# Two layers of attention and gated MLP on one core: shared score passes, zero-weight matmuls in idle TensorE slots, w_sp transposed once, and a spatial sum in four passes

## The chip, the cores and the metric

The kernel runs on one core of one Trainium2 chip. The metric is the device time of one launch in microseconds (us), as the median of several runs. The profile's span, from the first to the last instruction of the core, is about 2 us shorter (2191.0 us where the run took 2192.77). "Granted clock" is the share of TensorE's full clock that the chip allowed, averaged over a stretch; PE is TensorE, ACT is ScalarE, DVE is VectorE, SP is the engine that issues most DMAs (transfers between memories). PSUM is the memory that TensorE writes into, in banks. A "fill" is the group of score matmuls that fills PSUM for one exponential; a "value product" multiplies exponentials by V; "side work" is all else on TensorE: projections, the mixer, the spatial sum. "Warm" and "cold" stand for full and half clock. A "stretch" is a window of time, in us from the start of the span.

## The reference, cut to what matters

```python
# S = 2048 tokens, D = 512, 32 heads of 16, one key and value head shared by all; all bf16
def attention(x):                        # called on the layer-normed x, added to x
    q = (x @ wq).reshape(S, 32, 16)
    k = x @ wk;  v = x @ wv              # [2048, 16] each
    p = softmax(q . k * 16 ** -0.5)      # 32 x 2048 x 2048 scores
    return (p @ v).reshape(S, 512) @ wo
def mixer(x):                            # called on the layer-normed x, added to x
    z = gelu(x @ w_in)                   # [2048, 1792]
    z1, z2 = z[:, :896], layernorm(z[:, 896:])
    g = w_sp @ z2 + b_sp[:, None]        # w_sp is 2048 x 2048: the "spatial sum" over tokens
    return (z1 * g) @ w_out
x = x + attention(ln(x)); x = x + mixer(ln(x)); x = x + attention(ln(x)); x = x + mixer(ln(x))
```

Each layer has 134 million scores. The kernel treats them as 2048 blocks of 128 keys by 512 (query, head) columns; over two layers that is 4096 blocks, and every block needs an exponential.

## The kernel before

The program is generated in Python by a list scheduler. It knows a duration for every operation, simulates the five engines, and fixes the order of each engine's instructions. On the chip that order is static; semaphores only hold an instruction until its inputs are there.

Score blocks are filled by TensorE in PSUM and then take one of two ways. ScalarE takes groups of three or two blocks and applies its exponential; VectorE takes single blocks and builds an exponential from seven arithmetic operations on pairs of blocks.

```python
self.chunks = [512, 512, 512, 256, 128, 128]   # query tokens per chunk; the mixer of a chunk follows its attention
self.passes = [(0, 8, 1), (8, 12, 2)]          # spatial sum: token tiles 0-7 after chunk 1, 8-11 after chunk 2
self.s_fin = 12                                # the final pass sums tiles 12-15 and finishes the layer
self.ring = [(0, 3), (3, 2)]                   # PSUM banks of ScalarE's fills: 3 and 2, alternating
self.pvb = 6                                   # one bank for the value product
sc = self.sc = Sched([5, 7])                   # only two spare banks for all side work and VectorE's fills
sc.streams["pe"] = [self.fill_s, self.pv_s, self.dx_s]

def _qk(self, e, b, bank):                     # one score block: 32 rows of the array, row group j
    for s, kt in enumerate(b.unit.kts):
        ins = e.matmul(self.b32(bank)[:, s * n:(s + 1) * n], self.kT[32 * j:32 * j + 32, kt * 128:(kt + 1) * 128],
                       self.qs[32 * j:32 * j + 32, g.qslot, 0:n], tile_position=(32 * j, 0), start=True, stop=True)

# FillStream: ScalarE's 3 or 2 blocks (priority 0)      DexStream: VectorE's block by itself (priority 2.5)
o = sc.op("pe", lambda e: k.qk(e, b, j.bank.idx), 0.27, deps, 2.5, sem="dfill", job=j, first=True)

# ... spatial(): for every 256 tokens tc and every tile s of the pass, a transposing load of 64 KB
ld = self.dma(lambda e, sl=sl, s=s, tc=tc: e.dma_start_transpose(
    self.wsT[:, sl, :], self.w_sp_d[tc * 256:(tc + 1) * 256, s * 128:(s + 1) * 128]), self.last_ws[sl] or [], ...)
if final: todo.append(("b", None))             # the bias, as a matmul
if acc:   todo.append(("g", None))             # the earlier passes' sum gp, added with an identity matmul
todo += [("w", w) for w in ws]
# not final: DVE copies PSUM to gp.  final: DVE multiplies PSUM by z1, then the product with w_out
```

In the final pass of a layer one "group" is six 128x256 matmuls (bias, identity, four tiles); there are 56 per layer. A group of an earlier pass has no bias.

The softmax here doesn't subtract the row's maximum and nothing guards it: scores larger than these inputs give would overflow.

## Time and profile before

| before | |
|---|---|
| time | 2193.21 us median (2191.41 to 2195.01, 2 runs) |
| ScalarE busy, VectorE busy, TensorE busy | 80%, 82%, 87% |
| mean granted TensorE clock | 0.747 |
| blocks exponentiated by ScalarE, VectorE | 3570, 526 |
| TensorE's wait for w_sp loads | 43.1 us, 20.6 of it at the boundary and 22.5 at the end |

To find where the time goes I cut the span at four marks: the first exponential on ScalarE, the end of the first layer's last GELU, the last copy into V for the second layer (from then on the second attention runs freely), and the end of the second layer's last GELU.

| stage (us) | start | attention 1 | boundary | attention 2 | end | sum |
|---|---|---|---|---|---|---|
| before | 29.6 | 939.4 | 170.6 | 914.2 | 137.2 | 2191.0 |

The page of the kernel before: busy time of each engine with its share of the span, then lines of busy tenths in 40 equal slices of the span (PEclk: granted clock in tenths), then the chain of work that ended last.

```profile
PE 1910.1 (87%) x16492; PEld 722.1 (33%) x16580; DVE 1792.7 (82%) x3228; ACT 1759.3 (80%) x1544; POOL 58.9 (3%) x104
...
PE   7999897998799989987888888878897999899778
...
DVE  7988899988899998953359999989989998988423
ACT  7999899988999998942149999999989999978300
...
PEclk8555595556799997788885557866668998965879
...
PE 47%; ACT 30%; issue 11%; DVE 8%; SPq 2%; DMA 1%; POOL 1%; ACTq 0%; DVEq 0%
ACT Pa L1111 28%; PE ps_all L1321 16%; PE ps_all L1166 9%; PE ps_all L923 7%; PE ps_all L652 3%; PE ps_all L967 2%; PE ps_all L796 2%; PE ps_all L921 2%; PE ps_all L817 2%; DVE E L1272 2%; SPq L888 1%; PE ps_all L918 1%; ACT z2n L836 1%; DVE gp L936 1%; DMA wsT<-in_B_w_sp_dram 1%
```

ScalarE and VectorE show 9 for most of the two attentions, and fall to 1 to 4 in slices 22 to 24 and at the end: those are the boundaries. TensorE is 7 to 9 everywhere, but PEclk is 5 in the early part of both attentions, where attention runs without side work. A busy TensorE at half clock is not a fast one: 32x512 score matmuls last 0.605 us on average where the clock is 0.5, and 0.384 us where it is 1.0. The chain (shares of the span, by engine and then by line) is mostly TensorE and ScalarE handing over to each other.

Groups of instructions of the kernel before (busy us, mean ns | idle before, and who ended it). L1111 is ScalarE's exponential, L1321 the score matmul, L1272 the first of VectorE's seven operations:

```profile
L1111 ACT ACTIVATE Pa<-ps_all 128x1536 bf16<-128x1536 f32 (+2 forms) x1429 | 1646.1, 1265 | 132.8 <-PE ps_all L1321 116.4
L1321 PE MATMUL ps_all<-qs,kT 32*128 32x512 bf16 (+2 forms) x6148 | 835.5, 392 | 161.2 <-ACT Pa L1111 142.5
...
L1272 DVE TENSOR_SCALAR E<-ps_all 128x512 int32<-128x512 f32 x526 | 349.5, 684 | 44.3 <-PE ps_all L1321 42.6
```

ScalarE was held up 116.4 us by score matmuls, VectorE 42.6 us. From the view of waits, TensorE's matmuls and its loads of weights (PEld), each with total us, times and longest us:

```profile
PE ps_all L918 <- DMA wsT<-in_B_w_sp_dram: 43.1, 8, 8.9
PEld ps_all L918 <- DMA wsT<-in_B_w_sp_dram: 6.5, 1, 6.5
```

The timeline of TensorE near the end of the kernel (start, us, what; in brackets the idle time before it and its cause):

```profile
2064.64 0.60 PE L923 MATMUL ps_all<-wsT,z2n 128*128 128x256 bf16 x4
2065.08 0.27 PE L921 MATMUL ps_all<-gp,ident 128*128 128x256 bf16 x1
2065.19 0.60 PE L923 MATMUL ps_all<-wsT,z2n 128*128 128x256 bf16 x4
2074.71 0.37 PE L918 MATMUL ps_all<-b_11,ident 8*128 8x256 bf16 x1 [8.92 <-DMA wsT<-in_B_w_sp_dram]
2075.01 0.39 PE L921 MATMUL ps_all<-gp,ident 128*128 128x256 bf16 x1
2075.20 1.06 PE L923 MATMUL ps_all<-wsT,z2n 128*128 128x256 bf16 x4
2076.19 0.39 PE L918 MATMUL ps_all<-b_11,ident 8*128 8x256 bf16 x1
```

TensorE stands still 8.92 us for a transposing load, and the groups after the wait run at half clock: from one L918 to the next 1.48 us, where warm groups take 0.86 (41 of them in this trace).

### The profile page before, as it was taken

The numbers are of one execution on the slowest core, as the hardware profiler recorded it, in microseconds if no ns is written. First come the engines' busy times: TensorE is split into PE (matmuls) and PEld (weight loads), VectorE is DVE, ScalarE is ACT, GpSimd is POOL, SyncE is SP. The second block draws the span as 40 slices with busy tenths as digits, with TensorE's granted clock in tenths as the row PEclk, the third lists the DMA queues.
The fourth block names the chain that finished last, engine by engine and source line by source line (L and its number), as shares of the span: only waits on it lengthen the run. The fifth ranks groups of instructions, "written<-read, shape, count | busy, mean of one in ns | idle before, by whom it ended". The sixth has DMA issues, their size and how long they took to land.

```text
span 2191.0 us, 39478 instructions
## 1 busy us (share of the span) xinstructions
PE 1910.1 (87%) x16492; PEld 722.1 (33%) x16580; DVE 1792.7 (82%) x3228; ACT 1759.3 (80%) x1544; POOL 58.9 (3%) x104
## 2 busy tenths in 40 slices
PE   7999897998799989987888888878897999899778
PEld 3111221122244335554431112211222443465444
DVE  7988899988899998953359999989989998988423
ACT  7999899988999998942149999999989999978300
POOL 2000000000000000000000000000000000000000
PEclk8555595556799997788885557866668998965879
DMA  2000001000001010021100000010000110100312
GB/s 93 1 1 1 1 1 37 1 1 1 18 21 29 12 30 15 3 71 37 28 21 1 1 1 1 1 37 1 1 1 18 25 25 1 38 12 2 75 51 72
DMA packets 108402, 42.97 MB, mean 20 GB/s; under 512 B 79288, under 2 KB 107712, under 8 KB 108224
## 3 DMA queue, kind: packets, MB, share of 16 engines
q1 hardware_dynamic: 108224, 40.44, 7.2%
q8 instruction: 130, 2.13, 0.4%
q14 instruction: 48, 0.39, 0.1%
HBM read 14.19 MB, written 9.44 MB: 11 GB/s over the span
## 4 chain that ended last, share of the span: by engine, by line
PE 47%; ACT 30%; issue 11%; DVE 8%; SPq 2%; DMA 1%; POOL 1%; ACTq 0%; DVEq 0%
ACT Pa L1111 28%; PE ps_all L1321 16%; PE ps_all L1166 9%; PE ps_all L923 7%; PE ps_all L652 3%; PE ps_all L967 2%; PE ps_all L796 2%; PE ps_all L921 2%; PE ps_all L817 2%; DVE E L1272 2%; SPq L888 1%; PE ps_all L918 1%; ACT z2n L836 1%; DVE gp L936 1%; DMA wsT<-in_B_w_sp_dram 1%
## 5 line engine op out<-in xcount | busy, mean ns | idle before, releaser
L1111 ACT ACTIVATE Pa<-ps_all 128x1536 bf16<-128x1536 f32 (+2 forms) x1429 | 1646.1, 1265 | 132.8 <-PE ps_all L1321 116.4
L1321 PE MATMUL ps_all<-qs,kT 32*128 32x512 bf16 (+2 forms) x6148 | 835.5, 392 | 161.2 <-ACT Pa L1111 142.5
L1166 PE MATMUL ps_all<-Pa,V 128*32 128x512 bf16 (+2 forms) x5369 | 517.9, 396 | 7.5 <-DVE oT L675 4.6
L1321 PEld LDWEIGHTS ps_all<-qs,kT 32*128 32x128 bf16 x6148 | 224.0, 101 | 733.0 <-ACT Pa L1111 484.7
L1272 DVE TENSOR_SCALAR E<-ps_all 128x512 int32<-128x512 f32 x526 | 349.5, 684 | 44.3 <-PE ps_all L1321 42.6
L1306 DVE SCALAR_TENSOR_TENSOR Pd<-E 128x1024 uint16<-128x1024 int32 x263 | 319.6, 1215 | 0.6
L923 PE MATMUL ps_all<-wsT,z2n 128*128 128x256 bf16 x1792 | 281.2, 291 | 5.1 <-DVE E L1272 2.1
L1166 PE MATMUL ps_all<-Pd,V 128*32 128x512 bf16 (+2 forms) x775 | 263.1, 403 | 0.0
L1166 PEld LDWEIGHTS ps_all<-Pa,V 128*32 128x32 bf16 x5369 | 134.1, 103 | 339.2 <-issue 278.9
L923 PEld LDWEIGHTS ps_all<-wsT,z2n 128*128 128x128 bf16 x1792 | 173.9, 103 | 62.6 <-issue 22.2
L1301 DVE TENSOR_TENSOR E<-E 128x1024 f16<-128x1024 f16 x263 | 180.0, 684 | 2.5
L1304 DVE TENSOR_TENSOR E<-E 128x1024 f16<-128x1024 f16 x263 | 179.8, 684 | 2.4
L1295 DVE TENSOR_SCALAR E<-E 128x1024 f16<-128x1024 uint16 x263 | 179.7, 685 | 1.2
L945 DVE TENSOR_TENSOR E<-ps_all,z1s 128x512 bf16<-128x512 f32 (+1 forms) x64 | 39.9, 624 | 124.3 <-PE ps_all L923 115.1
L1298 DVE TENSOR_SCALAR E<-E 128x1024 f16<-128x1024 f16 x263 | 110.3, 420 | 2.4
L1297 DVE TENSOR_SCALAR E<-E 128x1024 f16<-128x1024 f16 x263 | 110.2, 419 | 1.3
L652 PE MATMUL ps_all<-xnTA,wq_pad 128*128 128x512 bf16 (+2 forms) x347 | 93.7, 383 | 11.7 <-issue 7.0
L542 ACT ACTIVATE xnTA<-ps_all 128x1024 bf16<-128x1024 bf16 x13 | 13.1, 1023 | 109.8 <-PE ps_all L533 109.8
L936 DVE CAST gp<-ps_all 128x512 bf16<-128x512 f32 (+1 forms) x128 | 78.4, 618 | 22.9 <-PE ps_all L923 22.3
L661 DVE CAST qs<-ps_all 128x512 bf16<-128x512 f32 (+2 forms) x94 | 47.6, 506 | 52.1 <-PE ps_all L652 51.7
L796 PE MATMUL ps_all<-w_in_r,xnTB 128*128 128x448 bf16 x256 | 77.5, 424 | 1.6 <-DVE E L1272 0.7
L918 PE MATMUL ps_all<-b_11,ident 8*128 8x256 bf16 x112 | 35.3, 315 | 48.9 <-DMA wsT<-in_B_w_sp_dram 43.1
(68 smaller groups left out, 1123.6 us busy)
## 6 DMA issues: line engine op xcount, KB each, us to landing
z1s<-z_scratch SPq DMA_DIRECT2D x16, 448.0 KB, 4.0
z_scratch<-z1s SPq DMA_DIRECT2D x6, 896.0 KB, 4.3
wsT<-in_B_w_sp_dram SPq DMA_TRANSPOSE x256, 2.4
X<-in_A_x_dram SPq DMA_DIRECT2D x8, 256.0 KB, 5.2
out_dram<-X SPq DMA_DIRECT2D x16, 128.0 KB, 1.9
w_in_r<-in_B_w_in_dram SPq DMA_DIRECT2D x1, 1792.0 KB, 9.9
E<-in_B_w_out_dram SPq DMA_DIRECT2D x2, 896.0 KB, 6.8
z_scratch<-z1s SPq DMA_DIRECT2D x2, 448.0 KB, 3.5
```

Source lines behind the costliest of these rows:

```text
L652: ins = e.matmul(self.b32(b)[:, 0:n], self.wq_pad[:, kd, g.hg, :], self.xnTA[:, kd, g.t0:g.t0 + n], start=(kd == 0), stop=(kd == KD - 1))
L796: ins = e.matmul(self.b32(b)[:, 0:448], self.xnTB[:, kd, i * 128:(i + 1) * 128], self.w_in_r[:, kd, FH + h * 448:FH + (h + 1) * 448], star ...
L923: ins = e.matmul(o_, self.z2n[:, w[0], f * 128:(f + 1) * 128], self.wsT[:, w[1], :], start=st, stop=sp_)
L1111: return e.activation(k.Pa[:, base:base + n, :], k.b32(b0, n).rearrange("p (k q) -> p k q", k=n), ACTF.Exp, scale=SCALE)
L1166: ins = e.matmul(k.b32(k.pvb)[32 * j:32 * j + 32, 0:n], k.V[:, kt, 32 * j:32 * j + 32], b.slot[:, s * n:(s + 1) * n], tile_position=(0, 32 ...
L1272: c = sc.op("dve", lambda e: e.tensor_scalar(k.eI[:, s, 512 * i:512 * (i + 1)], k.b32(j.bank.idx)[:, 0:512], C_LOG2, C_BIAS, op0=ALU.mult, ...
L1295: return lambda e: e.tensor_scalar(out, a, m, None, op0=ALU.mult)
L1298: return lambda e: e.tensor_scalar(out, a, m, b, op0=ALU.mult, op1=ALU.add)
L1301: o4 = sc.op("dve", lambda e: e.tensor_tensor(q, u, w, ALU.mult), d_sb(1024, 0.521e-3), [o3], pr)
L1304: o6 = sc.op("dve", lambda e: e.tensor_tensor(q, q, u, ALU.mult), d_sb(1024, 0.521e-3), [o5], pr)
L1306: o7 = sc.op("dve", lambda e: e.scalar_tensor_tensor(po.bitcast(U16), I, 2.0 ** -9, q, op0=ALU.mult, op1=ALU.add), d_sb(1024, 1.042e-3), [ ...
L1321: ins = e.matmul(self.b32(bank)[:, s * n:(s + 1) * n], self.kT[32 * j:32 * j + 32, kt * 128:(kt + 1) * 128], self.qs[32 * j:32 * j + 32, g ...
```

## The change

Its intent: keep TensorE's clock up through attention, take VectorE's separate score matmuls out of TensorE's time, and free the boundaries of transposing loads and left-over work. The core of the diff:

```diff
+TICK = 3.4133
+TICK_COLS = 3060.0
...   # the scheduler's model: below TICK_COLS array-weighted columns in a step, the next step is slow
+    def fast(self, t):
+        return self.tick.get(int(t / TICK) - 1, 0.0) >= TICK_COLS
...   # idle TensorE slots
+class WarmStream:
+        t = sc.below(f, TICK_COLS + WARM)        # WARM = 250
+        if not sc.fast(t):
+            return (t, -1.0)                      # cold: before everything else
+        return (t, 0.6)                           # warm: after fills and value products, before side work
+                ins = e.matmul(k.b32(k.pvb)[:, 0:n], k.zero[:], k.wo_r[:, 0, 0:n], start=False, stop=False)
...   # VectorE's block x joins ScalarE's fill, in a row group that the fill leaves free
+        x = k.dx_s.take(t, [b.j for b in blocks])
             for i, b in enumerate(blocks):
                 ins = k.qk(e, b, b0 + i)
+            if x is not None:
+                ins = k.qk(e, x, j.bank.idx)
-        o = sc.op("pe", lambda e: k.qk(e, b, j.bank.idx), 0.27, deps, 2.5, sem="dfill", job=j, first=True)
...   # w_sp: 16 transposes of 512 KB into the buffer gp, stored to DRAM, during chunk 0
+            tr = self.dma(lambda e, s=s: e.dma_start_transpose(stg[:, s % 7, :], self.w_sp_d[:, s * 128:(s + 1) * 128]), ...)
+            st = self.dma(lambda e, s=s: e.dma_start(self.ws_d.ap()[s], stg[:, s % 7, :]), [tr], ...)
...   # then plain loads of up to four tiles
-                ld = self.dma(lambda e, ...: e.dma_start_transpose(self.wsT[:, sl, :], ...))
+            ld = self.dma(lambda e, ...: e.dma_start(
+                self.wsT[:, 4 * sl:4 * sl + s1 - s0, :], self.ws_dv[:, s0:s1, tc * 256:(tc + 1) * 256]), ...)
...   # four passes; the middle ones add in SBUF with VectorE, no identity matmul
-        self.passes = [(0, 8, 1), (8, 12, 2)]
+        self.passes = [(0, 4, 0), (4, 8, 1), (8, 12, 2)]
-                    if acc:
+                    if final:
                         todo.append(("g", None))
+                        if acc:
+                            return e.tensor_tensor(dst, src, dst, ALU.add)
...   # small: value products wait to run in pairs, the first two query projections of a chunk get priority 0.8
...   # instead of 1.5, wk, wv and wq are loaded from ScalarE's queue, some modelled durations are corrected
```

## The prediction

The sum: about 60, 100 and 3, put at about 165 us.

> **What bounds the kernel now.** Two layers of attention, each followed by a gated MLP. Exponentials of the scores are split between ScalarE (1428 ACTIVATEs, 3570 blocks of 128x512; 1646 us busy, 461 ns a block) and VectorE (526 blocks in 263 chains; a chain's operations sum to about 5.4 us, 2.7 us a block). The page gives ScalarE 80% and VectorE 82% of 2191 us. Neither is full, for two reasons.

> **What the change does.**
> - Zero-weight 128x128x512 matmuls fill up to 3310 weighted columns per 3.41 us: two to three per step, 0.22 us each warm, 1000 to 1500 in all. [...] That zero weights count as work no trace here shows; I assume it (85%).
> - VectorE's score matmul shares the pass of ScalarE's in a free row group: about 500 separate matmuls (0.4 to 0.6 us each) vanish.
> - w_sp: 16 large transposes to DRAM during chunk 0, then plain loads. The waits of 27 and 22 us should nearly vanish.
> - Four passes with SBUF accumulation: 64 more VectorE evictions (0.69 us: 44 us of VectorE, worth about 6 us shared with ScalarE), 112 identity matmuls fewer; earlier passes finish inside attention.
> - Weight loads on ScalarE's queue: about 3 us at the start.

> **Critical path.** Attention: if ScalarE and VectorE rise to about 96 and 94%, 1845 us becomes about 1780, plus 6: saves about 60. Boundaries: 27 + 18 + about 10 of cold clock in the middle, 22 + 9 + about 15 at the end: about 100. Start: 3. Sum about 165: 2025 us. ScalarE's exponentials remain the limit; all-full engines would need about 1720 us of attention, so more is possible.

> **Predicted: 2025 us, 1950 to 2100.** Faster by over 2%: 0.94; within 2%: 0.04; slower: 0.02.

> **What would show it.** Mean granted clock over 0.9 (0.747 now); ScalarE's wait for score matmuls under 50 us; 32x512 score matmuls about 0.4 us; TensorE's wait for w_sp loads a few us; ScalarE idle at each boundary about 95 us instead of 135 to 145; VectorE blocks 520 to 570.

> **What would make it wrong.** Zero weights not counted: the clock stays low and the added matmuls delay fills. The large transposes landing late, so the first pass's evictions (into the same buffer) hold both spare PSUM banks. A paired fill waiting for VectorE's bank and stopping ScalarE. The schedule assuming a warm clock where it is cold.

## More of the kernel before

A stretch of the first attention without side work, from the view of stretches (busy us and number of instructions per engine, then clock, DMA share and GB/s):

```profile
core 0: us, PE busy (x) PEld busy (x) DVE busy (x) ACT busy (x) POOL busy (x), PEclk, DMA share, GB/s
60.00:200.00 140.00, 128.59 (x695) 25.87 (x696) 124.73 (x206) 130.48 (x113) 0.00 (x0) 0.50 0.00 1
```

Here the clock is 0.50, ScalarE is busy 93% (130.48 of 140) and VectorE 89%.

## The result, and the profile after

| | before | after |
|---|---|---|
| median | 2193.21 us (2 runs) | 2028.37 us (2025.82 to 2030.91, 2 runs) |
| ratio | | 0.9248, 95% interval 0.9189 to 0.9308 |
| mean granted clock | 0.747 | 0.928 |
| ScalarE, VectorE busy | 80%, 82% | 86%, 89% |
| blocks of VectorE | 526 | 519 |

The same kernel, run again later with five rounds, gave 2031.44 us and 0.9268 (0.9245 to 0.9291).

| stage (us) | start | attention 1 | boundary | attention 2 | end | sum |
|---|---|---|---|---|---|---|
| before | 29.6 | 939.4 | 170.6 | 914.2 | 137.2 | 2191.0 |
| after | 16.4 | 912.0 | 122.9 | 879.2 | 98.4 | 2028.9 |
| saved | 13.2 | 27.4 | 47.7 | 35.0 | 38.8 | 162.1 |

The two attentions save 62.4 us, the boundary and the end 86.5 us, the start 13.2 us. The page of the kernel after, the same lines:

```profile
PE 1683.5 (83%) x17285; PEld 674.8 (33%) x17285; DVE 1804.6 (89%) x3287; ACT 1745.4 (86%) x1528; POOL 58.7 (3%) x105
...
PE   7777788978798887879987787898888977878799
...
DVE  7999999999999999985459999999998999989654
ACT  7999999999998999991369999999999999999700
...
PEclk9999998989897898799988979989899999979799
...
DVE 32%; PE 32%; ACT 25%; issue 9%; DMA 1%; POOL 1%; SPq 0%; ACTq 0%
ACT Pa L1173 22%; PE ps_all L1429 8%; PE ps_all L957 7%; DVE E L1340 6%; DVE Pd L1378 5%; PE ps_all L1241 5%; DVE E L1373 3%; DVE E L1376 3%; DVE E L1367 3%; PE ps_all L1005 3%; PE ps_all L1416 2%; PE ps_all L853 2%; DVE E L1369 2%; DVE E L1370 2%; PE ps_all L704 1%
```

PEclk is 8 or 9 nearly throughout. ScalarE and VectorE are at 9 in almost every slice of attention, and TensorE, doing the zero-weight matmuls on top, is less busy than before. The chain is now shared: VectorE's part went from 8% to 32%, TensorE's from 47% to 32%. The stretch without side work:

```profile
60.00:200.00 140.00, 104.60 (x841) 26.05 (x842) 137.58 (x229) 138.22 (x123) 0.00 (x0) 0.96 0.20 50
```

The clock is 0.96 instead of 0.50; ScalarE is busy 98.7% and VectorE 98.3% (138.22 and 137.58 of 140). In this stretch hardly anything is left to win but fewer or shorter operations. The clock alone is not what fills the two engines here: the runs without zero-weight matmuls and without pairing, below, tell the two apart. The groups, with L1173, L1429 and L1340 in the places of L1111, L1321 and L1272, and L1416 the zero-weight matmul:

```profile
L1173 ACT ACTIVATE Pa<-ps_all 128x1536 bf16<-128x1536 f32 (+1 forms) x1431 | 1638.9, 1304 | 72.6 <-PE ps_all L1429 64.7
L1429 PE MATMUL ps_all<-qs,kT 32*128 32x512 bf16 (+2 forms) x6144 | 597.1, 331 | 262.1 <-ACT Pa L1173 240.4
...
L1340 DVE TENSOR_SCALAR E<-ps_all 128x512 int32<-128x512 f32 x519 | 351.3, 682 | 25.7 <-PE ps_all L1429 23.7
...
L1416 PE MATMUL ps_all<-wo_r,zero 128*128 128x512 bf16 (+2 forms) x821 | 218.4, 376 | 0.0
```

ScalarE's wait for score matmuls fell from 116.4 to 64.7 us, VectorE's from 42.6 to 23.7. The final pass in the timeline of TensorE:

```profile
1967.00 3.32 PE L957 MATMUL ps_all<-wsT,z2n 128*128 128x256 bf16 x28 [0.26 <-DVE gp L973]
1970.76 0.26 PE L952 MATMUL ps_all<-b_12,ident 8*128 8x256 bf16 x1 [0.44 <-DVE gp L973]
1970.96 0.28 PE L955 MATMUL ps_all<-gp,ident 128*128 128x256 bf16 x1
1971.08 0.60 PE L957 MATMUL ps_all<-wsT,z2n 128*128 128x256 bf16 x4
1971.61 0.28 PE L952 MATMUL ps_all<-b_12,ident 8*128 8x256 bf16 x1
```

No wait for a w_sp load is left in the view of waits, and groups follow each other at 0.85 us. The first line of the five is a sign that one hope failed: 28 matmuls without a bias matmul before them are seven groups of the pass over tiles 8 to 11, which should have been done in attention. Counted in the trace, 11 such left-over groups ran in the boundary and 38 at the end, against 29 and 35 before the change.

### The profile page after: what moved, and what is told of

Its sections match the earlier page's. It is cut to its first block, busy times and chain, and to the rows that moved or that the text cites. A ratio compares the mean times of both kernels' runs of the same rounds, so it can differ in the third digit from the quotient of the medians.

```text
span 2028.9 us, 41252 instructions
## 1 busy us (share of the span) xinstructions
PE 1683.5 (83%) x17285; PEld 674.8 (33%) x17285; DVE 1804.6 (89%) x3287; ACT 1745.4 (86%) x1528; POOL 58.7 (3%) x105
## 4 chain that ended last, share of the span: by engine, by line
DVE 32%; PE 32%; ACT 25%; issue 9%; DMA 1%; POOL 1%; SPq 0%; ACTq 0%
ACT Pa L1173 22%; PE ps_all L1429 8%; PE ps_all L957 7%; DVE E L1340 6%; DVE Pd L1378 5%; PE ps_all L1241 5%; DVE E L1373 3%; DVE E L1376 3%; DVE E L1367 3%; PE ps_all L1005 3%; PE ps_all L1416 2%; PE ps_all L853 2%; DVE E L1369 2%; DVE E L1370 2%; PE ps_all L704 1%
## 5 line engine op out<-in xcount | busy, mean ns | idle before, releaser
L1173 ACT ACTIVATE Pa<-ps_all 128x1536 bf16<-128x1536 f32 (+1 forms) x1431 | 1638.9, 1304 | 72.6 <-PE ps_all L1429 64.7
L1429 PE MATMUL ps_all<-qs,kT 32*128 32x512 bf16 (+2 forms) x6144 | 597.1, 331 | 262.1 <-ACT Pa L1173 240.4
L1429 PEld LDWEIGHTS ps_all<-qs,kT 32*128 32x128 bf16 x6144 | 177.1, 95 | 751.2 <-ACT Pa L1173 660.8
L1340 DVE TENSOR_SCALAR E<-ps_all 128x512 int32<-128x512 f32 x519 | 351.3, 682 | 25.7 <-PE ps_all L1429 23.7
L1241 PE MATMUL ps_all<-Pa,V 128*32 128x512 bf16 (+2 forms) x5366 | 352.8, 331 | 2.7 <-DVE oT L727 1.6
L1378 DVE SCALAR_TENSOR_TENSOR Pd<-E 128x1024 uint16<-128x1024 int32 (+1 forms) x260 | 315.3, 1213 | 0.8
L1416 PE MATMUL ps_all<-wo_r,zero 128*128 128x512 bf16 (+2 forms) x821 | 218.4, 376 | 0.0
L1373 DVE TENSOR_TENSOR E<-E 128x1024 f16<-128x1024 f16 (+1 forms) x260 | 177.3, 682 | 3.0
L1376 DVE TENSOR_TENSOR E<-E 128x1024 f16<-128x1024 f16 (+1 forms) x260 | 177.1, 681 | 2.3
L1367 DVE TENSOR_SCALAR E<-E 128x1024 f16<-128x1024 uint16 (+1 forms) x260 | 176.7, 681 | 1.1
L1370 DVE TENSOR_SCALAR E<-E 128x1024 f16<-128x1024 f16 (+1 forms) x260 | 108.4, 417 | 2.1
L1369 DVE TENSOR_SCALAR E<-E 128x1024 f16<-128x1024 f16 (+1 forms) x260 | 108.3, 416 | 1.5
L1416 PEld LDWEIGHTS ps_all<-wo_r,zero 128*128 128x128 bf16 x821 | 65.4, 104 | 105.9 <-issue 90.4
L973 DVE TENSOR_TENSOR gp<-ps_all,gp 128x512 bf16<-128x512 f32 (+1 forms) x128 | 77.9, 617 | 20.1 <-PE ps_all L957 19.4
L853 PE MATMUL ps_all<-xnTB,w_in_r 128*128 128x512 bf16 (+2 forms) x336 | 69.2, 326 | 6.8 <-DVE z1s L861 3.0
```

The costliest lines, as they stand in the source:

```text
L1173: return e.activation(k.Pa[:, base:base + n, :], k.b32(b0, n).rearrange("p (k q) -> p k q", k=n), ACTF.Exp, scale=SCALE)
L1241: ins = e.matmul(k.b32(k.pvb)[32 * j:32 * j + 32, 0:n], k.V[:, kt, 32 * j:32 * j + 32], b.slot[:, s * n:(s + 1) * n], tile_position=(0, 32 ...
L1340: return k.sc.op("dve", lambda e: e.tensor_scalar(k.eI[:, s, 512 * i:512 * (i + 1)], k.b32(j.bank.idx)[:, 0:512], C_LOG2, C_BIAS, op0=ALU. ...
L1367: return lambda e: e.tensor_scalar(out, a, m, None, op0=ALU.mult)
L1369: return lambda e: e.tensor_scalar(out, a, b, None, op0=ALU.add)
L1370: return lambda e: e.tensor_scalar(out, a, m, b, op0=ALU.mult, op1=ALU.add)
```

## The experiments

All kernels gave correct results. Twelve runs were made, in three or five rounds beside the kernel before (four or five timings each). "Attention" and "boundaries" are sums of the stages defined above, from the profiled run (attention 1 + 2; boundary + end).

| kernel | median us | ratio to before (95%) | clock | attention | boundaries |
|---|---|---|---|---|---|
| before | 2187 to 2193 | 1 | 0.75 | 1853.6 | 307.8 |
| after | 2028.37 | 0.9248 (0.9189 to 0.9308) | 0.928 | 1791.2 | 221.3 |
| no zero-weight matmuls | 2101.27 | 0.9600 (0.9566 to 0.9633) | 0.750 | 1852.2 | 230.9 |
| zero-weight matmuls on 1/16 of the array | 2160.18 | 0.9872 (0.9841 to 0.9903) | 0.762 | 1926.6 | 220.5 |
| no pairing | 2108.88 | 0.9638 (0.9594 to 0.9682) | 0.903 | 1852.2 | 233.4 |
| old w_sp path | 2050.48 | 0.9368 (0.9322 to 0.9413) | 0.930 | 1790.1 | 246.6 |
| no pairing, old w_sp path | 2168.35 | 0.9908 (0.9883 to 0.9933) | 0.890 | 1868.3 | 285.6 |
| pairing as two groups | 2041.00 | 0.9317 (0.9286 to 0.9348) | 0.929 | 1805.6 | 217.6 |
| no pairing, VectorE's fills first | 2130.65 | 0.9740 (0.9703 to 0.9777) | 0.885 | 1883.6 | 240.8 |
| after, repeated | 2031.44 | 0.9268 (0.9245 to 0.9291) | 0.938 | 1788.1 | 220.0 |
| bias in the first pass | 2017.93 | 0.9209 (0.9181 to 0.9237) | 0.922 | 1815.8 | 189.5 |
| zero-weight matmuls last | 2023.00 | 0.9237 (0.9214 to 0.9260) | 0.927 | 1810.3 | 198.8 |
| both of these | 2019.33 | 0.9213 (0.9187 to 0.9240) | 0.928 | 1819.5 | 185.2 |
| both, and a fifth pass | 2030.08 | 0.9261 (0.9234 to 0.9289) | 0.934 | 1827.2 | 187.0 |

The theory before the first runs: the clock gives most of the gain in attention, the w_sp path most of it at the boundaries, pairing little. The rival: pairing and the better-informed schedule give the gain, and the clock only follows. What the expectations call the gate stands for what the clock records show, steps of 3.41 us at 0.5 or at 1.0; what decides between the two was to be tested.

### Without the zero-weight matmuls

```diff
-        sc.streams["pe"] = [self.fill_s, self.pv_s, WarmStream(self)]
+        sc.streams["pe"] = [self.fill_s, self.pv_s]
```

> The changed kernel without the zero-weight matmuls, all else kept. Theory (the clock gate gives most of the gain in attention): mean granted clock falls from 0.93 to about 0.8, ScalarE's wait for score matmuls rises from 65 to over 100 us, and the time rises by 40 to 70 us, to about 2085. Rival (the paired fill and the better schedule give the gain, the clock only follows): within 15 us of the changed kernel's 2028.

Measured: 2101.27 us, 73 us slower than the changed kernel, clock 0.750, ScalarE's wait for score matmuls 89.1 us. Of 71 us in the profiled runs, 61 are lost in attention, which is as long as before the change (1852.2 against 1853.6 us). The rival falls for the time; the expected wait and the expected clock (0.8) were set too high. Note that the clock is no higher than before the change, and yet the kernel is 4.0% faster than before: the rest of the change works without the clock. The stretch without side work shows it:

```profile
60.00:200.00 140.00, 115.46 (x728) 22.06 (x728) 136.34 (x227) 134.55 (x118) 0.00 (x0) 0.57 0.20 53
```

At a clock of 0.57, ScalarE is busy 96% (134.55 of 140) and VectorE 97%, nearly as much as with the zero-weight matmuls. Their 73 us are earned almost wholly after it: when 256 of the 4096 blocks are exponentiated, this run is 3 us behind the changed kernel, and 71 at the end.

### Zero-weight matmuls on a corner of the array

The schedule is the same instruction for instruction; only the area of the zero-weight matmuls differs.

```diff
-ins = e.matmul(k.b32(k.pvb)[:, 0:n], k.zero[:], k.wo_r[:, 0, 0:n], start=False, stop=False)
+ins = e.matmul(k.b32(k.pvb)[0:32, 0:n], k.zero[0:32, 0:32], k.wo_r[0:32, 0, 0:n],
+               tile_position=(0, 0), start=False, stop=False)
```

> The changed kernel with every zero-weight matmul kept in its place and as long, but on a 32x32 corner of the array (1/16 of the area). Theory (the gate weighs columns by the share of the array in use): the clock is as low as without them, about 0.8, and the time is that of no zero-weight matmuls or worse, 2085 to 2110. Rival (the gate only asks whether TensorE is occupied): clock 0.93 and 2028 us, as the changed kernel.

Measured: 2160.18 us and a clock of 0.762; the forecast of 2085 to 2110 was too low, its direction right. The zero-weight matmuls are all there, and the groups show what they do to the others:

```profile
PEclk9556678967795688789975557888677956777699
...
L1173 ACT ACTIVATE Pa<-ps_all 128x1536 bf16<-128x1536 f32 (+1 forms) x1431 | 1666.1, 1254 | 179.9 <-PE ps_all L1430 163.9
...
L1340 DVE TENSOR_SCALAR E<-ps_all 128x512 int32<-128x512 f32 x519 | 353.7, 686 | 80.9 <-PE ps_all L1430 79.3
...
L1416 PE MATMUL ps_all<-wo_r,zero 32*32 32x512 bf16 (+2 forms) x821 | 278.1, 455 | 0.0
```

PEclk is back to 5 to 7 in attention, and ScalarE waits 163.9 us for score matmuls, more than before the change. This is the cleanest of the experiments, since only the area differs: occupation of TensorE with little area brings hardly any clock (0.762 against 0.750 without these matmuls) and costs 59 us against not having them at all (2160.18 less 2101.27). With the full area the same schedule is 132 us faster (2160.18 less 2028.37).

The rule can also be tested without a run. The clock records are steps of 3.41 us at 0.5 or at 1.0. I summed in every step the matmul columns, each weighted by (rows x columns used) / (128 x 128), and asked whether the next step is at 1.0 when the sum is at least 3000. Over the whole trace this misjudges 37 of 636 steps before the change (the prediction, counted a little differently, had 38 of 637) and 33 of 589 after. If in the trace after the change the zero-weight matmuls are left out of the sum, it misjudges 173, and about 80 with the threshold that then suits best, hardly fewer than if every step were called warm (86); so zero weights count. If columns are not weighted by area at all, the best possible threshold still misjudges 186 steps before the change; weighted by the rows in use alone, or by the columns of the array in use alone, over 100. Much of what the rule gets wrong lies at the edges of steps: with a matmul that crosses an edge shared between the two steps, it misjudges 22 steps of 637 before, 8 of 590 after, and 15 of 629 in the run with 1/16 of the area.

### Without pairing

VectorE's score matmuls are again a stream of their own, with the code of before; zero-weight matmuls and w_sp path stay.

```diff
-        sc.streams["pe"] = [self.fill_s, self.pv_s, WarmStream(self)]
+        sc.streams["pe"] = [self.fill_s, self.pv_s, self.dx_s, WarmStream(self)]
-        x = k.dx_s.take(t, [b.j for b in blocks])
+        x = None
# DexStream as before the change: own operation on TensorE, priority 2.5
```

> The changed kernel with VectorE's score matmuls issued by themselves again, as a stream of low priority (as before the change); the zero-weight matmuls and the w_sp path kept. Theory (pairing is a small part, since a warm TensorE has room): 10 to 30 us slower, about 2048; VectorE's wait for its score matmul rises from 24 toward 43 us. Rival (pairing gives most of the gain in attention): 50 us slower or more.

Measured: 2108.88 us, 80 us slower. My theory, that pairing is a small part, falls; the rival's size is what came. Pairing is worth as much as the zero-weight matmuls, and without either of them attention is back at 1852 us. (The edit also brings back the old stream's choice of blocks and its modelled durations; no run has those alone.) VectorE's wait for its own score matmuls is 63.7 us, ScalarE's for score matmuls 93.2. The stretch without side work shows something more:

```profile
60.00:200.00 140.00, 123.94 (x736) 27.26 (x735) 116.52 (x193) 123.28 (x108) 0.00 (x0) 0.74 0.19 51
```

The zero-weight matmuls are there (1064 in the trace of the whole run, 821 with pairing), but the clock is only 0.74 in this stretch, against 0.96 with pairing, and ScalarE (88%) and VectorE (83%) are below the kernel before. An explanation from the numbers of this stretch, not shown by a run of its own, goes by passes: matmuls that start within 30 ns of each other count as one (in the changed kernel three score matmuls start 3 ns apart at 151.699 us, and each takes 0.385 us). A score matmul that runs alone takes a whole pass of 512 columns and adds only 128 weighted ones (32 of 128 rows). At half clock the trace of before shows two such matmuls starting 427 ns apart (the first at 43.564 us), so a step of 3.41 us holds at most 8 passes, 4096 columns (estimate). Counted in the two traces, both stretches run passes of 4007 columns a step; without pairing these weigh 3202, with pairing 3586. A cold TensorE that must do the separate matmuls would then have little room for the area that warms it.

But a warm clock alone does not replace pairing. The run without pairing and with the old w_sp path, below, reached 0.85 in the same stretch, and ScalarE (92%) and VectorE (89%) are no fuller than before the change at 0.50:

```profile
60.00:200.00 140.00, 114.33 (x770) 28.28 (x780) 123.98 (x205) 128.53 (x113) 0.00 (x0) 0.85 0.00 1
```

With pairing and no zero-weight matmuls they were at 96% and 97% with a clock of 0.57. In this stretch, then, pairing is what fills the engines.

### VectorE's separate fills first

Is it the place in line? The run without pairing again, with VectorE's fills before value products and side work.

```diff
-        return (max([d.vis for d in deps] + [bf]), 2.5)
+        return (max([d.vis for d in deps] + [bf]), 0.3)
```

> As the run without pairing, but VectorE's separate score matmuls go before the value matmuls and all side work (priority 0.3 instead of 2.5). Theory A (separate issue costs because VectorE's fills stand behind other TensorE work and VectorE starves): VectorE's wait for score matmuls falls below 30 us and the time to within 25 us of 2028. Theory B (it costs TensorE time, so whoever goes first the other waits): stays at 2085 to 2120, with ScalarE's wait for score matmuls at or over 93 us.

Measured: 2130.65 us. VectorE now gets its fills: its wait is 34.1 us, it does 562 blocks instead of 512. But ScalarE pays:

```profile
L1173 ACT ACTIVATE Pa<-ps_all 128x1536 bf16<-128x1536 f32 (+1 forms) x1414 | 1631.0, 1267 | 170.6 <-PE ps_all L1434 113.7 <-PE ps_all L1238 51.7
...
L1349 DVE TENSOR_SCALAR E<-ps_all 128x512 int32<-128x512 f32 x562 | 367.5, 683 | 35.4 <-PE ps_all L1434 34.1
```

Its waits for TensorE are 113.7 us for score matmuls and 51.7 for value products. Theory A falls. Theory B holds in kind, though the time lies above its 2085 to 2120: the separate matmuls cost TensorE time that somebody has to wait for, whoever goes first (for score matmuls ScalarE waits 113.7 us and VectorE 34.1 here, 93.2 and 63.7 in the run before).

### Pairing as two groups

The same block at the same place, but as an operation of its own behind ScalarE's group, with its own wait and semaphore.

```diff
-            if x is not None:
-                ins = k.qk(e, x, j.bank.idx)
...
+            ox = k.sc.op("pe", lambda e: k.qk(e, x, j.bank.idx), 0.05, k.dx_s.deps(x), 0.0, sem="dfill", cols=128,
+                         slow=0.05, job=j, first=True)
+            k.sc.commit(ox, k.sc.free["pe"])
-            if x.unit is u:
+            if x.unit is u or x.unit.index == self.u + 1:      # close a half batch in time
```

> The changed kernel with VectorE's score matmul as a group of its own right behind ScalarE's group (own wait, own semaphore, same place, same block); to keep the schedule from locking up, a half batch is also closed when the next unit needs it. Theory A (what counts is the place: at once with ScalarE's fill, in a free row group, where the array overlaps it anyway): within 20 us of 2028. Theory B (what counts is being one group with one wait): near the 2108 of separate issue.

Measured: 2041.00 us, 10 to 13 us slower than the two measurements of the changed kernel, 68 us faster than separate issue. So theory A holds: what counts is being next to ScalarE's fill. In the trace of the changed kernel matmuls in different row groups run at the same time: at 151.699 us three score matmuls start 3 ns apart and each takes 0.385 us. Counted in the traces (starts within 80 ns of the one before are one pass), the 3072 score matmuls of 512 columns make 1363 passes before the change, 1382 without pairing, 1082 after it, and 1093 in this run. Whether the remaining 10 to 13 us are the second wait, the half batches closed early or just another static schedule is open.

### The old w_sp path

```diff
-        self.passes = [(0, 4, 0), (4, 8, 1), (8, 12, 2)]
+        self.passes = [(0, 8, 1), (8, 12, 2)]
# the 16 large transposes and stores removed; the spatial sum with 64 KB transposing loads and identity matmuls restored
```

> The changed kernel with the spatial sum of before: transposing loads of 64 KB, three passes with identity matmuls; zero-weight matmuls and pairing kept. Theory (the w_sp path gives the gain at the boundaries, about 68 us between the same marks): 40 to 65 us slower, about 2080, TensorE waits 35 to 50 us for these loads, attention itself no longer. Rival (warmth and pairing shorten the boundaries, since more of the earlier passes fits into attention): under 20 us slower.

Measured: 2050.48 us, 22 us slower. The boundaries are 25 us longer, attention is not (1790.1 against 1791.2). The expectation of 40 to 65 us falls; the rival's "under 20" is nearly met. TensorE's wait for these loads is there, but small:

```profile
PE ps_all L941 <- DMA wsT<-in_B_w_sp_dram: 11.1, 3, 4.9
```

It is 11.1 us instead of the 43.1 of the kernel before, with the very same loads. So most of what the boundaries gained (61 of 86 us: 307.8 less 246.6) did not need the new path. In this kernel TensorE is idle for 26.7 us in the two boundary stages, in the kernel before for 64.8, in the changed kernel for 15.2. Why the same loads delayed less is not settled: the scheduler now counts 0.5 us for issuing a DMA where it counted 0.06 (in the trace of before the 256 loads of 64 KB held SP's queue 1.10 to 2.40 us each, 1.24 us in the median; eight in a row took 11.1 us from 2062.28 us), and their order in that queue is another one. Neither can be the whole of it: without pairing (next run), with the same loads and the same 0.5 us, TensorE waits 25.6 us for them.

### No pairing and the old w_sp path

```diff
# both edits above together; zero-weight matmuls stay
```

> The changed kernel with pairing and the w_sp path both undone, so what is left of the change is the zero-weight matmuls and small schedule corrections. Additive theory: 80 + 22 us over the changed kernel, about 2130, clock about 0.9. Rival (warmth and pairing need each other, since separate score matmuls and zero-weight matmuls compete for TensorE): 2150 or more. Rival (either is enough by itself): under 2100.

Measured: 2168.35 us, 0.9908 of before. The additive theory fails, and the rival's 2150 or more came: with pairing and the new path undone, zero-weight matmuls and the small corrections together gain 0.9%, although the clock is 0.890. Attention is even longer than before the change (1868.3 against 1853.6 us). With the other parts present the same matmuls are worth 3.5 points (0.9600 less 0.9248). Whether they lack pairing, as the rival says, or the w_sp path, these runs do not separate; the w_sp path too is worth more without pairing (0.9908 less 0.9638, 2.7 points) than with it (0.9368 less 0.9248, 1.2). The worth of the small corrections alone, and of pairing without anything else, is not measured.

The boundaries, too, depend on pairing: with the old path they take 285.6 us without it and 246.6 with it. Groups of the earlier passes left over into boundary and end are 44 and 53 without it, 15 and 36 with it, and TensorE is idle there for 41.9 us instead of 26.7.

### Bias in the first pass

```diff
-                    if final:
+                    if not acc:
                         todo.append(("b", None))
```

> A candidate: the bias matmul of the spatial sum moves from the final pass to the first one, inside attention. At the boundaries a group of six matmuls took 0.86 us with it and 0.55 us without, 56 groups a layer: 17 us a boundary, so 25 to 34 us faster than the changed kernel, about 2000. If the boundaries are not bound by TensorE: under 8 us faster.

Measured: 2017.93 us, 0.9209. The boundaries are 32 us shorter, as computed from the groups. But attention is 25 us longer (1815.8 against 1791.2), so only about 10 us remain: less than the 25 to 34 forecast. The boundaries are bound by TensorE, as that forecast assumed; it left out what attention would pay.

### The changed kernel again, and three candidates

> The changed kernel unaltered, on the chip of the three candidates of this call: 0.925 of the kernel before, within 0.006, about 2025 us.

Measured: 0.9268, 2031.44 us. In the next three kernels the zero-weight matmuls stand behind real side work while the clock is warm. The first of them also closes half batches (a pair of VectorE's blocks of which only one is filled) early, as the run with two groups did.

```diff
-        return (t, 0.6)
+        return (t, 4.5)
```

> The changed kernel with the zero-weight matmuls put behind all real side work (priority 4.5 instead of 0.6) as long as the clock is warm; when it is cold they still go first. A half batch is also closed when the next unit needs it, without which the schedule locks up. Theory (zero-weight matmuls push the earlier spatial passes out of attention into the boundaries, where 12 and 38 groups of them still ran): fewer are needed, the left-over groups fall under half, boundaries 10 us shorter in sum, time 5 to 15 us less. Rival (what holds the passes back is spare PSUM banks and VectorE, not TensorE): left-over groups and time unchanged within 10 us.

Measured: 2023.00 us. The left-over groups fell from 11 and 38 to 7 and 6, and the boundaries by 21 us, as the theory said; the rival's unchanged groups did not come. But the theory's cause is not shown: in the next kernel, with the same priority, 0 and 38 groups are left, and in the run without any zero-weight matmuls 30 and 45, more than with them. What keeps the passes out of attention is open. Attention took 22 us more and gave it back in the profiled run; by the medians 8 us are left, and the intervals overlap.

> The run with the bias in the first pass and the zero-weight matmuls behind real side work. Bias alone shortened the boundaries by 32 us and lost 25 in attention. If that loss came from zero-weight matmuls queuing with the added side work: about 2000 us, 0.913 of the kernel before. If the loss is the chance of another static schedule: anywhere from 2000 to 2025.

Measured: 2019.33 us, 0.9213 (0.9187 to 0.9240), 12 us less than the changed kernel in the same rounds, whose interval (0.9245 to 0.9291) it does not touch. It is no faster than the bias alone. The first of the two expectations, about 2000, falls; the second, 2000 to 2025, is met.

```diff
-        self.passes = [(0, 4, 0), (4, 8, 1), (8, 12, 2)]
-        self.s_fin = 12
+        self.passes = [(0, 4, 0), (4, 8, 1), (8, 12, 2), (12, 14, 3)]
+        self.s_fin = 14
```

> As the run before, and the last pass split: tiles 12 and 13 are summed after the fourth chunk, so the final pass has two of four matmuls less a group (56 groups, 0.22 us: 12 us a boundary less TensorE work, if the added pass finishes in time). Gain over the run before: 10 to 20 us. If the added pass is left over into the boundary: none, as its 64 evictions then stand there.

Measured: 2030.08 us, no gain over the changed kernel and 11 us slower than the kernel just before it. Boundaries 187.0, attention 1827.2. The second of the two cases came: 52 and 48 of the 56 groups of the added pass were left over into boundary and end.

The four candidates have one pattern: boundaries 21 to 35 us shorter than in the repeated run, attention 22 to 39 us longer in the profiled runs. The work that leaves the boundaries goes into attention, where TensorE is 82% busy by the trace. Whether each of these microseconds was paid for by TensorE's time there, or partly by another static schedule, the runs do not tell: the schedule of the pairing in two groups did the same work and its attention was 14 us longer. The bias in the first pass, alone or with the zero-weight matmuls last, is the best version that ran, 0.4 to 0.6% faster than the changed kernel.

## Why the prediction was right

The predicted time was 2025 us, the measured 2028. The sum is better than its terms.

- **Attention, 60 us.** Right in size: 62.4 us between the marks used here. ScalarE went from 91.9% to 94.4 and 95.1% in the two attentions, VectorE from 89.3% to 94.4 and 93.8% (predicted 96 and 94). But the prediction gave a price only to the fuller engines and put the clock first; it listed pairing without a value. The runs show that taking away either one costs 73 or 80 us, and that the parts do not add up: the zero-weight matmuls are worth 3.5 points with pairing and the new w_sp path, and with the small corrections together only 0.9 without.
- **Zero weights count as work** (assumed, 85%): shown, by the clock of 0.928 against 0.762 with the same schedule and 1/16 of the area, and by the sorting of steps, which fails without them (173 misjudged steps instead of 33).
- **How many zero-weight matmuls.** The step "1000 to 1500 in all" failed: the trace has 821, and 318 of them (821 less 503) are the shorter 256 and 128 column forms. I had taken attention's own weighted columns from a slower kernel; a faster one does more per step by itself (from 60 to 200 us, 2297 a step before and 2587 after, zero-weight matmuls left out).
- **Boundaries, 100 us.** Too large: 86.5. Two terms failed. "Earlier passes finish inside attention", worth 18 and 9 us, did not come true: 11 and 38 groups were still left, against 29 and 35. Why is open: the candidates first pointed to the zero-weight matmuls, but without any of them 30 and 45 are left. And the 27 us of waiting in the middle counted one wait twice, 20.6 us of the matmuls plus the same wait's 6.5 us as the weight load sees it. The claim that the waits of 27 and 22 us should nearly vanish was right, none is left, but its cause was given too simply: with the old loads kept the waits already fall from 43.1 to 11.1 us, and the new path is worth 22 us of time.
- **Start, 3 us.** Too small: the first exponential comes 13.2 us earlier. I counted only the loads on ScalarE's queue and overlooked the raised priority of the first query projections. Every experiment kept both and started at 15.4 to 17.4 us, so no run separates them, but the traces do: ScalarE's first copy of K starts 1.2 us earlier than before (13.77 against 15.01 us), and the first queries are copied at 15.24 us, straight after it, where before they came at 28.33 us, behind all of K and V. About 12 of the 13.2 us are this order.
- **Checks set in advance.** Clock over 0.9: 0.928. Score matmuls of 512 columns at about 0.4 us: 0.408 on average. ScalarE's wait under 50 us: 64.7, missed. ScalarE idle at each boundary about 95 us: 82 (122.9 us at 33% busy) and 98. VectorE blocks 520 to 570: 519, missed by one. Evictions 64 more and identity matmuls 112 fewer: as counted.
- **The feared failures** did not come: the large transposes and stores were issued between 17 and 78 us, long before the first pass.

So the total was right partly by luck: a start 10 us better than written made up for boundaries 13 us worse. The mechanism of attention was half right: the clock rises as forecast, but pairing, which had no price in the sum, is worth as much.

## What to carry to other kernels

When TensorE's clock follows its recent work, count that work as array area per step, from the clock records of your own trace: idle slots can then be filled on purpose, with full-array matmuls (1/16 of the area gave a clock of 0.762, all of it 0.928). Merge passes that use little of the array first: here, in the stretch without side work, that filled both exponential engines to 96% and more at a clock of 0.57, and a clock of 0.85 without it did not. In that stretch, with zero-weight matmuls on the full array, the clock was 0.74 to 0.85 in the three runs without pairing and 0.90 to 0.96 in the four with it whose stretch was read. Before moving work out of a bound stage, ask what the stage that takes it has free (TensorE was 82% busy in attention): here 32 us less at the boundaries cost 25 us in attention. Take a change apart in both directions, because its parts here were worth 0.9 or 3.5 points depending on what else was present, and a right total can hide wrong terms. Before adding two lines of waits, look whether they are one wait seen by two engines.
